# The query projection of a two-part decode attention kernel: unrolled matmuls against a loop with register addresses

## The chip, the cores and the metric

The kernel runs on one core of a Trainium2 chip. The metric is device time in microseconds (us) of one execution. A trace is one profiled execution; its span is about 1.5 us shorter than the time of the same run (245.4 against 246.84 us in the kernel before). Ratios are the mean time of one kernel's fast runs over the mean of the other's fast runs of the same rounds, so they differ a little from the ratio of the medians that stand beside them.

## The reference

Two independent attention layers for one new token, A and B. A sees only the last 2048 keys of its cache, B sees all 8192. The outputs are concatenated.

```python
# x: 1 x 576, wq: 576 x 4096, caches: 16 heads x 8192 x 128, wo: 4096 x 576, all bf16
q = (x @ wq).reshape(32 heads, 128)
k, v = the cache (A: its last 2048 rows), each head used by two query heads
p = softmax(q @ k.T * 128 ** -0.5)
out = (p @ v).reshape(4096) @ wo
```

Nearly all of the bytes are K and V (B: 64 MiB, A: 16 MiB) and the four weight matrices (4.5 MiB each). Each byte is loaded once.

## The kernel before

Five groups of K and V (group 0 is A, groups 1 to 4 are B) pass through four SBUF slots of 4 MiB each: two for K, two for V. SyncE issues all large loads into one queue. Ahead of the groups stand the two query projections. Their weights borrow slots that the groups will need: B's wq covers the second K slot, so the load of A's second K half may be issued only when the last q matmul of B has read its weights.

```python
    WQ = [(4 * SLOT - WQ_W, [("v", 0, 1), ("v", 1)]),                       # A's wq: in the V slots
          (SLOT, [("k", 1, 0), ("k", 1, 1), ("v", 0, 0)])]                  # B's wq: in the second K slot
    for P in range(2):
        off, res = WQ[P]
        x_columns(P)                 # VectorE spreads x over the weight columns of the matmuls
        load(slots[:, off:off + WQ_W], ... wqs[P] ..., res, "wq%d" % P)
        q_part(P, off, res)          # 36 matmuls
        q_finish(P)                  # ScalarE copy, 4 small matmuls, VectorE copy
    # (cut)
    for g in range(NG):              # NG = 5
        for s in range(2):
            load_kv(ks, g, s, koff(s), KS[s], "k")
        # (cut: V loads, transposes of K, scores, softmax, V, all on TensorE in one loop over g)
```

One q part, before the change:

```python
    def q_part(P, off, res):
        def mm(pe):
            for u in range(9):
                for j in range(4):
                    o = off + u * 2048 + j * 512
                    ins = pe.matmul(opsum[32 * j:32 * j + 32, P * 512:(P + 1) * 512], lhsT=xpad[:, P, u, :],
                                    rhs=slots[:, o:o + 512], start=(u == 0), stop=(u == 8))
            return ins
        add("pe", mm, reads=[("xpad", P)] + res, writes=[B_O[P]])
```

## Time and profile before

| | before |
|---|---|
| time, median | 247.23 us in 3 runs before the prediction; 247.14 us with the 3 runs beside the changed kernel |
| bytes moved | 102.8 MB at 419 GB/s |
| TensorE (PE) busy | 67% of the span |
| q matmuls of B end, second K load issued | 26.8 us, 26.83 us |
| packets, in order of start, reach the last byte of the first K half (about where the queue would have ended) | 33.86 us |

From the page of the kernel before: busy tenths of PE and of the DMA engines in 40 slices of 6.1 us each, the bytes moved per slice, and the head of the chain of waits that ended last.

```profile
PE   0006329993836999443999390999671699859684
...
DMA  9998999999999999999999999999999999999993
GB/s 349 421 445 383 426 425 421 418 418 419 469 419 433 438 423 427 427 438 427 427 434 443 438 433 433 427 427 427 433 433 427 433 438 433 427 445 427 403 416 140
...
DMA 8%; PE 3%; DVE 0%; SPq 0%; issue 0%
```

The DMA engines work all the time, and the chain ends in a load. PE has gaps everywhere. The kernel takes as long as its bytes take, so PE work is free as long as it never lets the queue run empty (run 10 below: the transposes start 8.8 us later, the queue stays full, and the time is 246.87 us).

The timeline of PE around the q parts (start, duration, engine, line, operation, output<-inputs, count, idle time before and what ended it). Line 433 is the q part, 444 its small follow-up, 472 the transposes of the first K half.

```profile
17.79 0.17 PE L415 MATMUL misc<-xnine,twice 64*128 64x18 bf16 x1 [17.79 <-DMA xnine<-in_B_x_dram]
18.77 4.03 PE L433 MATMUL opsum<-slots,xpad 128*32 128x512 bf16 x36 [0.81 <-DVE xpad L424]
23.50 0.26 PE L444 MATMUL misc<-selq,qrow 128*128 128x8 bf16 x4 [0.70 <-ACT qrow L439]
24.66 2.13 PE L433 MATMUL opsum<-slots,xpad 128*32 128x512 bf16 x36 [0.91 <-DMA slots<-in_B_wq_dram]
...
35.07 2.18 PE L472 MATMUL ktps<-ident,slots 128*128 128x128 bf16 x19 [7.33 <-PEq L214]
```

After q, PE idles for 7.3 us at its wait in line 214: it waits for the first K half, whose last packets are only then on their way. The timeline of SyncE shows how the DMA queue is fed:

```profile
26.83 2.48 SPq L404 DMA_DIRECT2D slots<-in_A_k_cache_dram  x4
29.36 12.76 SPq L404 DMA_DIRECT2D slots<-in_A_v_cache_dram  x8
```

The issue at 26.83 us comes right after the last q matmul. The queue had work until about 33.9 us at that moment, so several microseconds were in hand.

### The profile page before, as it was taken

Reading aid. Unit: us, or ns where it says so; the run is one execution under the profiler, and the core shown is the slowest. Engines: PE = TensorE matmul, PEld = TensorE weight load, DVE = VectorE, ACT = ScalarE, POOL = GpSimd, SP = SyncE. Lnnn points to the kernel's source line nnn. Section 1 sums busy time; section 2 is a strip of 40 time slices with the busy share of each in tenths; the row PEclk is TensorE's granted clock in tenths of the full one; section 3 lists DMA queues with packets and bytes.
Section 4 is the critical chain, followed back from the end, with each engine's and each line's share of the span. In section 5 each row is a group of like instructions: output and inputs, shape, how many; then the busy total and the mean of one; then the engine's idle time right before and its main releaser. Section 6 shows DMA issues by size and latency. Waiting matters only on the chain. (4 is left out here: it accounts for less than half of the span.)

```text
span 245.4 us, 5175 instructions
## 1 busy us (share of the span) xinstructions
PE 165.1 (67%) x2285; PEld 117.5 (48%) x2285; DVE 87.2 (36%) x148; ACT 87.4 (36%) x95; POOL 10.7 (4%) x48
## 2 busy tenths in 40 slices
PE   0006329993836999443999390999671699859684
PEld 0002129781316876213877130978330687625463
DVE  0001205654142465250556323355524256533311
ACT  2000016873003786101778200577600378610000
POOL 7400000000000000000000000000000000000000
PEclk9999957999575999795899866599979599975679
DMA  9998999999999999999999999999999999999993
GB/s 349 421 445 383 426 425 421 418 418 419 469 419 433 438 423 427 427 438 427 427 434 443 438 433 433 427 427 427 433 433 427 433 438 433 427 445 427 403 416 140
DMA packets 5796, 102.87 MB, mean 419 GB/s; under 512 B 794, under 2 KB 924, under 8 KB 1180
## 3 DMA queue, kind: packets, MB, share of 16 engines
q1 hardware_dynamic: 5628, 102.77, 98.2%
q8 instruction: 5, 0.08, 0.1%
q10 hardware_dynamic: 160, 0.00, 0.0%
q14 instruction: 3, 0.02, 0.0%
HBM read 102.76 MB, written 0.00 MB: 419 GB/s over the span
## 5 line engine op out<-in xcount | busy, mean ns | idle before, releaser
L478 ACT ACTIVATE kt<-ktps 128x1024 bf16<-128x1024 bf16 x80 | 78.5, 1022 | 95.1 <-PE ktps L472 94.9
L472 PE MATMUL ktps<-ident,slots 128*128 128x128 bf16 x1280 | 89.1, 236 | 34.1 <-PEq L214 34.1
L472 PEld LDWEIGHTS ktps<-ident,slots 128*128 128x128 bf16 x1280 | 83.2, 107 | 49.7 <-issue 49.7
L481 DVE COPY kt<-ktps 128x1024 bf16<-128x1024 bf16 x80 | 55.3, 692 | 74.1 <-PE ktps L472 74.1
L546 PE MATMUL opsum<-slots,ptm 128*32 128x512 bf16 x320 | 32.0, 557 | 5.1 <-PEq L214 5.1
L493 PE MATMUL sacc<-kt,qst 128*32 128x512 bf16 x320 | 25.4, 392 | 1.9 <-PEq L214 1.9
L546 PEld LDWEIGHTS opsum<-slots,ptm 128*32 128x32 bf16 x320 | 13.0, 127 | 18.9 <-issue 16.8
L557 DVE TENSOR_TENSOR vtmp<-opsum,maskV 128x512 f32<-128x512 f32 x8 | 5.5, 692 | 22.6 <-PE opsum L546 22.6
L415 PE MATMUL misc<-xnine,twice 64*128 64x18 bf16 x1 | 0.2, 173 | 17.8 <-DMA xnine<-in_B_x_dram 17.8
L524 PE MATMUL misc<-ident,psb 128*128 128x128 bf16 x40 | 3.3, 230 | 11.6 <-PEq L214 11.6
L462 POOL COPY qst<-qcol 128x8 bf16<-128x8 bf16 x20 | 3.1, 191 | 163.7 <-PE sacc L493 149.3
L439 ACT ACTIVATE qrow<-opsum 128x512 bf16<-128x512 f32 x2 | 1.2, 597 | 22.7 <-PE opsum L433 22.7
L524 PEld LDWEIGHTS misc<-ident,psb 128*128 128x128 bf16 x40 | 2.5, 101 | 14.0 <-issue 14.0
L640 PE MATMUL ktps<-slots,opj 128*32 128x144 bf16 (+1 forms) x192 | 8.3, 271 | 1.1 <-DMA slots<-in_B_wo_dram 1.1
L514 ACT ACTIVATE psb<-sacc,stat 128x1024 bf16<-128x1024 f32 x5 | 5.6, 1114 | 9.5 <-DVE stat L508 9.5
L493 PEld LDWEIGHTS sacc<-kt,qst 128*32 128x32 bf16 x320 | 5.0, 94 | 7.9 <-issue 4.3
L415 PEld LDWEIGHTS misc<-xnine,twice 64*128 64x128 bf16 x1 | 0.1, 103 | 17.8 <-issue 17.8
L533 DVE TENSOR_SCALAR ptm<-misc,par 128x512 bf16<-128x512 bf16 x10 | 4.4, 480 | 10.4 <-PE misc L524 10.4
L640 PEld LDWEIGHTS ktps<-slots,opj 128*32 128x32 bf16 x192 | 6.2, 104 | 3.1 <-DMA slots<-in_B_wo_dram 1.5
L384 DVE TENSOR_REDUCE acc<-vtmp 128x128 f32<-128x1024 f32 x4 | 7.5, 1872 | 0.1
L433 PE MATMUL opsum<-slots,xpad 128*32 128x512 bf16 x72 | 6.2, 504 | 1.7 <-DMA slots<-in_B_wq_dram 0.9
L424 DVE TENSOR_SCALAR xpad<-misc,par 128x5 bf16<-128x5 f32 (+1 forms) x8 | 1.2, 230 | 14.0 <-PE misc L415 14.0
(65 smaller groups left out, 41.2 us busy)
## 6 DMA issues: line engine op xcount, KB each, us to landing
slots<-in_B_k_cache_dram SPq DMA_DIRECT2D x8, 4096.0 KB
slots<-in_B_v_cache_dram SPq DMA_DIRECT2D x8, 4096.0 KB
slots<-in_A_k_cache_dram SPq DMA_DIRECT2D x8, 1024.0 KB
slots<-in_A_v_cache_dram SPq DMA_DIRECT2D x8, 1024.0 KB
slots<-in_A_wq_dram SPq DMA_DIRECT2D x1, 4608.0 KB, 13.6
slots<-in_B_wq_dram SPq DMA_DIRECT2D x1, 4608.0 KB, 23.7
slots<-in_A_wo_dram SPq DMA_DIRECT2D x1, 4608.0 KB, 19.2
slots<-in_B_wo_dram SPq DMA_DIRECT2D x1, 3024.0 KB, 26.0
```

Of the source, the lines that this page charges most:

```text
L384: add("dve", lambda dve: dve.tensor_reduce(out, view, AX.X, ALU.add), reads=reads, writes=writes, tag=tag)
L433: ins = pe.matmul(opsum[32 * j:32 * j + 32, P * 512:(P + 1) * 512], lhsT=xpad[:, P, u, :], rhs=slots[:, o:o + 512], start=(u == 0), stop=( ...
L472: ins = pe.matmul(ktps_bf[q][:, t * 128:(t + 1) * 128], lhsT=slots[:, o:o + 128], rhs=ident[:, :], start=True, stop=True, is_transpose=True)
L478: add("act", lambda act, q=q, dst=dst: act.activation(dst, ktps_bf[q], ACT.Copy), reads=[("bank", q)], writes=[("kt", u % NKT, q)], tag="e ...
L481: add("dve", lambda dve, q=q, dst=dst: dve.tensor_copy(dst, ktps_bf[q]), reads=[("bank", q)], writes=[("kt", u % NKT, q)], tag="e%d%d" % ( ...
L493: ins = pe.matmul(sacc[32 * j:32 * j + 32, :], lhsT=qst[:, o:o + 32], rhs=rhs, start=(u == 0 and e == 0), stop=True, skip_group_check=True)
L514: return act.activation(psb[:, :].rearrange("p (x g) -> p x g", g=2), src, ACT.Exp, bias=st(C_NB + g), scale=SCALE, accum_out=st(C_L + g))
L524: ins = pe.matmul(dst[:, t * 128:(t + 1) * 128], lhsT=psb[:, t * 128:(t + 1) * 128], rhs=ident[:, :], start=True, stop=True, is_transpose= ...
L533: ins = dve.tensor_scalar(to, src, par2[:, e:e + 1], None, ALU.mult)
L546: ins = pe.matmul(opsum[32 * j:32 * j + 32, s * 512:(s + 1) * 512], lhsT=ptm[:, o:o + 32], rhs=v[:, :, b:b + 128], start=(tt == 0), stop=( ...
L557: add("dve", lambda dve: dve.tensor_tensor(vtmp[:, 4 * s:4 * s + 4, :], src, by, ALU.mult), reads=[B_O[s], w], writes=[("vtmp", s)], tag=" ...
L640: ins = pe.matmul(ktps[P][32 * j:32 * j + 32, 0:w], lhsT=opj[:, P, jj:jj + 32], rhs=slots[:, o:o + w], start=(jj == 0), stop=(jj == HQ - 1))
```

## The change

Intent: a shorter PE program. Seven of the nine units of each q part run as passes of a loop, whose weight and data addresses are computed into registers. The first and the last unit stay static, because they carry the flags and the signal. The output address is always static; the helper takes a static matmul and gives it the inputs of a register-addressed one.

```diff
+    def by_register(pe, second):
+        block = nc.cur_bb.bb.instructions
+        first = block.pop()
+        second()
+        other = block.pop()
+        return pe.add_instruction(copy.replace(first, ins=other.ins, name=nc.get_next_instruction_name()))
+
     def q_part(P, off, res):
+        def one(pe, j, part, w, x, start):
+            return pe.matmul(opsum[part:part + 32, P * 512:(P + 1) * 512], lhsT=w, rhs=x[:, j * 512:(j + 1) * 512],
+                             start=start, stop=True, skip_group_check=True)
+
         def mm(pe):
-            for u in range(9):
+            w, x = xpad[:, P, :, :].rearrange("p u c -> p (u c)"), slots[:, off:off + WQ_W]
+            for j in range(4):
+                one(pe, j, 32 * j, w[:, 0:32], x[:, 0:2048], True)
+            with pe.Fori(1, 8) as u:
+                wu, xu = w[:, bass.ds(u * 32, 32)], x[:, bass.ds(u * 2048, 2048)]
                 for j in range(4):
-                    o = off + u * 2048 + j * 512
-                    ins = pe.matmul(opsum[32 * j:32 * j + 32, P * 512:(P + 1) * 512], lhsT=xpad[:, P, u, :],
-                                    rhs=slots[:, o:o + 512], start=(u == 0), stop=(u == 8))
+                    one(pe, j, 32 * j, w[:, 0:32], x[:, 0:2048], False)
+                    by_register(pe, lambda: one(pe, j, 0, wu, xu, False))
+            for j in range(4):
+                ins = one(pe, j, 32 * j, w[:, 8 * 32:9 * 32], x[:, 8 * 2048:9 * 2048], False)
             return ins
```

## The prediction

> **What bounds the kernel now.** The DMA engines. The page's DMA row reads 9 in nearly every slice, 102.8 MB move at 419 GB/s, and the chain of waits ends in an 18.5 us transfer of B_wo. TensorE is busy 67%: work on it costs nothing until it leaves the DMA queue empty.

> **Where the q matmuls stand.** In the timeline, the 36 matmuls of q for A run from 18.8 to 22.8 us (0.107 us apart[...]), those of B from 24.66 to 26.79 us (0.059 us apart). Only then may the second half of A's K be loaded, because B's wq lies in those slots: SyncE issues it at 26.83 us. Until then the queue holds only the rest of A's first K half, whose last packet ends at 33.86 us (packet records). The kernel's first packets came 1.0 us after their issue. So the end of q for B can slip by about 5.7 us for free. What it slips beyond that is DMA idle time, and as the queue never runs dry afterwards, it comes out one for one at the end.

> **What the change removes.** 96 static weight loads and matmuls, less 20 added instructions: about 10 per q part, of which 4 are the loop's own and about 6 compute addresses. Static instructions are cheap: the sequencer passed some 72 between 18.74 and 19.62 us, 12 ns each. The trace has five 16 KB instruction fetches on one queue, 1 us each; none repeats per pass of the outer loop and none delays the chain. I expect no gain.[...]

> **What it adds.** Seven passes per q part. The outer loop's records price control: register move to next move 0.103 us, add to branch 0.10 us, taken branch to the next record 0.27 us: 0.47 us per pass. Six more register operations at 0.10 us: 0.6 us. Eight register-addressed instructions (4 weight loads, 4 matmuls): nothing in this trace has such an operand[...]. Sum about 1.5 us per pass (0.9 to 2.2), against 0.43 or 0.24 us of array time now. The sequencer sets the pace.

> **On the critical path.** q for A ends at 18.75 + 0.2 + 7 x 1.5 + 0.5 = 30 us; q for B starts 1.85 us later (as now) and ends at about 43 us. The K issue moves from 26.8 to 43 us; DMA idles from 33.9 to about 44: some 10 us.

> **Prediction.** 257.5 us, 80% range 248.5 to 267. Faster by over 2%: 3%; within 2%: 20%; slower by over 2%: 77%.

> **What would show each step.** The DMA row falls to near 0 for a slice or two around 34 to 44 us. Each q part shows groups of 4 matmuls about 1.5 us apart. SyncE's second K issue is near 43 us. PE's transposes start near 44 instead of 35.07 us. From 80 us on all is shifted by one constant.

> **What would make it wrong.** A pass under 0.8 us: the slack swallows it and the time stays at 247. Fewer address operations[...].[...]

The sum in "What it adds" came to about 1.5 us per pass, the two terms that stand make 0.47 + 0.6 = 1.07 us, and the rest, about 0.43 us, was for the eight register-addressed instructions, of which the trace before had none.

## The result, and the profile after

The changed kernel takes 250.76 us (median of 6 runs, 250.54 to 251.08), the kernel before 247.14 us (6 runs): ratio 1.0141, 95% interval 1.0125 to 1.0157. It is slower, by about a third of what was forecast.

The same rows of the page of the changed kernel (slices of 6.2 us):

```profile
PE   0008679499442999490999580799764599859684
...
DMA  9998949999999999999999999999999999999993
GB/s 331 426 461 376 425 176 389 418 427 424 423 449 452 436 422 425 420 425 425 467 416 441 425 425 425 420 462 425 441 425 425 420 425 436 452 446 408 422 415 135
...
DMA 7%; PE 3%; DVE 0%; SPq 0%; issue 0%
```

One slice stands out: the sixth of the DMA row, 31 to 37 us, reads 4 where 9 stood, and 176 GB/s. The rest looks as before. The timelines of PE and of SyncE show the cause; line 440 is the q part now, 491 the transposes.

```profile
19.13 4.23 PE L440 MATMUL opsum<-slots,xpad 128*32 128x512 bf16 x20 [0.81 <-DVE xpad L426]
23.59 0.76 PE L440 MATMUL opsum<-slots,xpad 128*32 x4 [0.23 <-issue]
24.60 0.76 PE L440 MATMUL opsum<-slots,xpad 128*32 x4 [0.26 <-issue]
25.59 1.06 PE L440 MATMUL opsum<-slots,xpad 128*32 x8 [0.23 <-issue]
...
34.94 1.06 PE L440 MATMUL opsum<-slots,xpad 128*32 x8 [0.24 <-issue]
...
36.99 0.22 PE L491 MATMUL ktps<-ident,slots 128*128 128x128 bf16 x1
```

```profile
36.04 2.48 SPq L406 DMA_DIRECT2D slots<-in_A_k_cache_dram  x4
38.57 6.72 SPq L406 DMA_DIRECT2D slots<-in_A_v_cache_dram  x8
```

The groups of four matmuls start 1.0 us apart, with 0.23 to 0.26 us in between in which PE waits for nothing that the profile shows ("issue"); the records of PE's sequencer, shown further below, fill that time. B's part ends at 36.0 us instead of 26.8, and the second K load is issued at 36.04 us. The stretches of both traces around it (length, busy time and count of each engine, granted PE clock, DMA share, GB/s), before and then after:

```profile
30.00:34.00 4.00, 0.00 (x0) 0.00 (x0) 0.00 (x0) 0.00 (x0) 0.00 (x0) 0.50 1.01 422
34.00:38.00 4.00, 2.93 (x28) 2.96 (x29) 0.69 (x1) 1.20 (x2) 0.00 (x0) 0.50 1.02 426
```

```profile
30.00:34.00 4.00, 3.52 (x17) 1.55 (x16) 0.00 (x0) 0.00 (x0) 0.00 (x0) 0.69 0.92 381
34.00:38.00 4.00, 3.02 (x35) 1.99 (x36) 0.98 (x5) 0.96 (x2) 0.00 (x0) 1.00 0.20 43
38.00:42.00 4.00, 4.00 (x68) 3.30 (x66) 3.24 (x5) 3.51 (x4) 0.00 (x0) 1.00 1.00 406
```

Between 34 and 38 us the DMA engines moved 43 GB/s instead of 426. The packet records give the edges: the last packet of the first K half ends at 34.67 us, the next load's first packet starts at 37.36 us. Counting landed bytes, the changed kernel reaches 13.7 MB 4.2 us later than the kernel before (38.20 against 34.03 us), 40 MB 4.1 us later, 90 MB 4.0 us later and 102 MB 4.1 us later. So the whole loss arises in this one gap, and none of it is made up or added to afterwards. (The profiled run of the changed kernel was its slowest, 251.08 us, and that of the kernel before a quick one, 246.84 us; hence 4.1 us here against 3.6 us between the medians.)

### The profile page after: what moved, and what is told of

Same layout as the page of the kernel before. It is cut to its first block, busy times and chain, and to the rows that moved or that the text cites. A ratio compares the mean times of both kernels' runs of the same rounds, so it can differ in the third digit from the quotient of the medians.

```text
span 249.5 us, 5275 instructions
## 1 busy us (share of the span) xinstructions
PE 170.1 (68%) x2285; PEld 117.7 (47%) x2285; DVE 87.0 (35%) x148; ACT 87.0 (35%) x95; POOL 10.7 (4%) x48
## 5 line engine op out<-in xcount | busy, mean ns | idle before, releaser
L491 PE MATMUL ktps<-ident,slots 128*128 128x128 bf16 x1280 | 86.2, 232 | 31.3 <-PEq L216 31.3
L491 PEld LDWEIGHTS ktps<-ident,slots 128*128 128x128 bf16 x1280 | 80.2, 105 | 46.7 <-issue 46.5
L440 PE MATMUL opsum<-slots,xpad 128*32 (+1 forms) x72 | 13.4, 475 | 3.4 <-DVE xpad L426 1.7
L543 PE MATMUL misc<-ident,psb 128*128 128x128 bf16 x40 | 4.0, 261 | 11.5 <-PEq L216 11.5
L440 PEld LDWEIGHTS opsum<-slots,xpad 128*32 (+1 forms) x72 | 5.9, 96 | 10.4 <-issue 9.1
L543 PEld LDWEIGHTS misc<-ident,psb 128*128 128x128 bf16 x40 | 3.0, 115 | 14.0 <-issue 14.0
L659 PEld LDWEIGHTS ktps<-slots,opj 128*32 128x32 bf16 x192 | 5.7, 103 | 3.5 <-DMA slots<-in_B_wo_dram 2.2
```

Of the source, the lines that this page charges most:

```text
L440: return pe.matmul(opsum[part:part + 32, P * 512:(P + 1) * 512], lhsT=w, rhs=x[:, j * 512:(j + 1) * 512], start=start, stop=True, skip_gro ...
L491: ins = pe.matmul(ktps_bf[q][:, t * 128:(t + 1) * 128], lhsT=slots[:, o:o + 128], rhs=ident[:, :], start=True, stop=True, is_transpose=True)
L543: ins = pe.matmul(dst[:, t * 128:(t + 1) * 128], lhsT=psb[:, t * 128:(t + 1) * 128], rhs=ident[:, :], start=True, stop=True, is_transpose= ...
L659: ins = pe.matmul(ktps[P][32 * j:32 * j + 32, 0:w], lhsT=opj[:, P, jj:jj + 32], rhs=slots[:, o:o + w], start=(jj == 0), stop=(jj == HQ - 1))
```

## The experiments

The theory: a q part delays only the issue of the second K load. Up to a limit this is free; beyond it the queue is empty and every microsecond counts. From the result, the limit is an issue at about 32.2 us (36.04 less 3.6 to 4.1). Rivals: each loop costs its share wherever it stands; taken branches are dear; matmuls with register addresses are dear; the shifted program costs time in other stages, by fetches.

The comparison with the reference called all ten runs correct, also the four with a wrong q (twice, fixed_address, fresh, apart_fresh). So it is blind to q here and proves nothing about the register addresses. Each group of runs shared its runs of the kernel before: medians 246.98 us (runs 1 to 4), 247.00 us (5 to 8) and 246.91 us (9 and 10).

### 1 and 2: one loop at a time

In loop_a, B's part is static; in loop_b, A's is (the condition is then `P == 0`).

```diff
         def mm(pe):
+            if P == 1:
+                # the nine static units, as in the kernel before
+                return ins
             w, x = xpad[:, P, :, :].rearrange("p u c -> p (u c)"), slots[:, off:off + WQ_W]
```

> Only A's q part runs in the loop; B's is unrolled as before. Theory (slack): a delay of the second K issue costs nothing until the queue runs dry; the changed kernel issued it at 36.0 us and lost 3.6 to 4.1 us, so the free limit is an issue at about 32.2 us. Here q for A ends near 26.3 us, q for B near 31 us (30 to 32.1), the K issue follows at once: loss 0 to 0.2 us, time 247.2 us, no gap in the DMA records. Rival (each loop costs its half, wherever it stands): 249.0 us.

Measured: 247.69 us (4 runs, 246.98 to 247.81), ratio 1.002, interval 1.0004 to 1.0037. The K issue came at 30.32 us and the DMA engines were never all idle there, though between 33.5 and 35 us only 311 GB/s landed (431 in the kernel before).

> Only B's q part runs in the loop. Theory (slack): q for B starts at 24.6 us and takes 7.5 us, the K issue is at about 32.1 us, just at the limit of 32.2 us: loss 0 to 0.3 us, time 247.2 to 247.5 us. Rival (half each): 249.0 us.

Measured: 247.24 us (247.09 to 247.28), ratio 1.001, interval 0.9993 to 1.0026. The K issue came at 32.30 us.

What follows: half the loops do not cost half the loss. One loop delays the K issue from 26.83 us by 3.5 us (loop_a) or 5.5 us (loop_b) and costs about 0.5 or 0.2 us by the ratios; two delay it by 9.2 us and cost 3.6 us. That is a threshold, but not a sharp one. loop_a was expected to lose at most 0.2 us and lost about 0.5 us (interval 0.1 to 0.9), more than loop_b, whose issue was later. Its trace reaches 13.7 MB 0.35 us late, without a gap. The same small delay stands in loop_b (0.41 us) and in run 7, no_loop (0.35 us), and at 102 MB all three are still 0.37 or 0.38 us late; run 8, two_units, shows only 0.07 us, although its issue was later than that of loop_a. What loop_a's trace loses beyond loop_b's arises in the last 0.1 MB of the queue. Neither is explained.

### 3 and 4: no K load waits for q of B

B's wq moves into the buffer of the transposed keys, which is unused until the q parts are over (it grows by 4 KiB per partition). The diff is abridged: the matmuls of B also read their weights from there. Done to the kernel before (apart_before) and to the changed one (apart_after).

```diff
-    kt = nc.alloc_sbuf_tensor("kt", [128, NKT, UNIT], BF16)
+    ktw = nc.alloc_sbuf_tensor("ktw", [128, WQ_W], BF16)
+    kt = ktw[:, 0:NKT * UNIT].rearrange("p (a y) -> p a y", a=NKT)
...
-    WQ = [..., (SLOT, [("k", 1, 0), ("k", 1, 1), ("v", 0, 0)])]
+    WQ = [..., (None, [("kt", u, q) for u in range(NKT) for q in range(4)] + ["ktw"])]
...
-        load(slots[:, off:off + WQ_W], ...
+        load(slots[:, off:off + WQ_W] if P == 0 else ktw[:, :], ...
```

> The kernel before, with B's wq in the buffer of the transposed keys (free until the q parts are over), so that no K load waits for q. Theory: the queue was never dry there anyway, so nothing is gained: 247.1 us (246.8 to 247.4). All K and V loads that wait for q parts now wait for A's part at most.

Measured: 247.00 us (246.85 to 247.29), ratio 1.0005, interval 0.9988 to 1.0021.

> The changed kernel with the same move of B's wq. Theory (the whole loss is the DMA gap at the second K load): gap gone, second K issue within the first 8 us, time as apart_before within 0.4 us: 247.2 us, though q for B still ends at 36 us. Rival (the loop or the shifted code costs time elsewhere, in fetches or in PE stages): stays near 250.7 us, or between.

Measured: 246.86 us (246.82 to 246.92), ratio 0.9995 to the kernel before, interval 0.9979 to 1.0012. Its q loops are as slow as ever. The timeline of PE in apart_after (line 441 is the q part, 492 the transposes), and its stretch of 34 to 38 us:

```profile
34.66 1.07 PE L441 MATMUL opsum<-ktw,xpad 128*32 x8 [0.24 <-issue]
36.42 0.26 PE L464 MATMUL misc<-selq,qrow 128*128 128x8 bf16 x4 [0.70 <-ACT qrow L459]
36.72 3.92 PE L492 MATMUL ktps<-ident,slots 128*128 128x128 bf16 x64
```

```profile
34.00:38.00 4.00, 3.02 (x40) 2.05 (x38) 1.25 (x5) 1.24 (x2) 0.00 (x0) 1.00 1.01 422
```

What follows: with the same loops, the same shorter program and q of B again ending near 36 us, but with the K load issued at 3.88 us, the loss is gone. The gap in the queue is the whole loss. The shorter program neither costs nor gains anything that these intervals (0.17% each way) can show.

### 5: each register-addressed matmul twice

```diff
-                for j in range(4):
+                for j in (0, 1, 2, 3, 0, 1, 2, 3):
```

> Wrong result on purpose: each pass of both loops issues its four register-addressed matmuls twice. In the changed kernel's trace one such matmul takes 0.124 us of the sequencer, so a pass should grow from 1.02 to 1.52 us, the value the prediction had used. Theory: 14 passes, so the K issue moves by 7.0 us from 36.0 to 43 us and the time by as much: 257.7 us (256.9 to 258.5). Rival (part of a longer gap is made up later): below 256 us.

Measured: 250.85 us (250.81 to 251.03), ratio 1.0158. The expectation failed, and the failure is the most telling result. The group of line 440 in the changed kernel, then in twice (PEldq is PE's sequencer):

```profile
L440 PEld LDWEIGHTS opsum<-slots,xpad x72: 91/93/103, 19.1 to 35.6; 128*32 x56, 128*32 128x32 bf16 x16
...
L440 PEldq FUSED_REGOPS  x56: 42/46/51, 19.4 to 35.2; - x56
```

```profile
L440 PEld LDWEIGHTS opsum<-slots,xpad x128: 92/93/112, 18.8 to 35.4; 128*32 x112, 128*32 128x32 bf16 x16
...
L440 PEldq FUSED_REGOPS  x56: 42/46/51, 19.1 to 35.1; - x56
```

There are 56 more matmuls, but the same 56 register operations: the second four matmuls found their addresses ready in registers. The mean distance between a pass's branch and the next is 1.017 us in both traces. So fifty-six extra matmuls with register addresses cost no measurable time. What costs is computing a fresh address; run 9 tests that.

### 6: the loop with constant addresses

```diff
-                wu, xu = w[:, bass.ds(u * 32, 32)], x[:, bass.ds(u * 2048, 2048)]
                 for j in range(4):
-                    one(pe, j, 32 * j, w[:, 0:32], x[:, 0:2048], False)
-                    by_register(pe, lambda: one(pe, j, 0, wu, xu, False))
+                    one(pe, j, 32 * j, w[:, 32:64], x[:, 2048:4096], False)
```

> Wrong result on purpose: both loops stay, but their matmuls have constant addresses, so no register operation but the count and the branch is left. Sum of records: add 0.10, branch 0.27, eight static instructions 0.10: a pass of 0.45 to 0.5 us. K issue near 29 us, under the limit of 32.2 us: 247.1 us. Rival (a taken branch is dear by itself[...]): passes near 1 us, 249 us or more.

Measured: 247.05 us (246.84 to 247.16), ratio 0.9999. A pass took 0.38 to 0.42 us in the records, less than expected, and the K issue came at 28.39 us. In A's part that is no longer than the four matmuls took in the kernel before (4 x 0.107 = 0.43 us). In B's part they had taken 4 x 0.059 = 0.24 us, so the loop costs something there, but the issue is only 1.56 us later and stays within the slack. The branch alone is harmless here.

### 7: register addresses without a loop

```diff
-            with pe.Fori(1, 8) as u:
+            count = pe.alloc_register("count%d" % P)
+            pe.reg_mov(count, 1)
+            for k in range(7):
+                u = pe.snap(count, min_val=1, max_val=7)
                 # (wu, xu and the four matmuls as in the changed kernel)
+                pe.reg_add(count, count, 1)
```

> Right result: both parts unrolled, but each of the 7 middle units takes its addresses from a register, as in the changed kernel. No branch: a unit should take 0.62 to 0.75 us. K issue at 30.5 to 32 us, at or under the limit: 247.1 to 247.4 us. Rival (register-addressed matmuls are dear[...]): 1.0 us per unit and 249.5 us or more.

Measured: 247.12 us (247.04 to 247.26), ratio 1.0006, interval 0.9989 to 1.0023. A unit took 0.70 to 0.74 us (one took 0.88), the upper end of what was expected: the first register operation of a unit, which by the author's reading takes in the count, lasted 142 to 153 ns instead of 78. The K issue came at 32.29 us, a little later than expected, at the limit. So neither the loop alone nor the addresses alone cost the 3.6 us; only their sum crosses the limit.

### 8: two units per pass

```diff
-            with pe.Fori(1, 8) as u:
-                wu, xu = w[:, bass.ds(u * 32, 32)], x[:, bass.ds(u * 2048, 2048)]
+            with pe.Fori(1, 7, 2) as u:
+                for k in range(2):
+                    wu, xu = w[:, bass.ds(u * 32 + 32 * k, 32)], x[:, bass.ds(u * 2048 + 2048 * k, 2048)]
...
-            for j in range(4):
-                ins = ...                        # unit 8
+            for k in range(7, 9):
+                for j in range(4):
+                    ins = ...                    # units 7 and 8
```

> Right result: the loop runs 3 passes of 2 units, one more unit is static; the program is still shorter than before, by about half as much. A pass: 1.02 us plus four matmuls at 0.124 us, about 1.52 us, so a part costs 3 x 1.52 instead of 7 x 1.02 us. K issue near 31.7 us, under the limit of 32.2 us: 247.2 us (247.0 to 247.6). Rival (any loop there costs): 249 us or more.

Measured: 246.96 us (246.66 to 247.18), ratio 0.9997, interval 0.9981 to 1.0014. A pass took 1.55 us, the K issue came at 31.67 us. This keeps a good part of the shortening (20 of 36 matmuls per part in the program instead of 12) at no cost. It does not beat the kernel before; no version here does, and none is to be expected to by this route, since the queue was never empty before.

### 9 and 10: longer passes, with fresh addresses

Because run 5 had not lengthened the pass, four matmuls with four new addresses were added to each.

```diff
                     by_register(pe, lambda: one(pe, j, 0, wu, xu, False))
+                next = x[:, bass.ds(u * 2048 + 2048, 2048)]
+                for j in range(4):
+                    one(pe, j, 32 * j, w[:, 0:32], x[:, 0:2048], False)
+                    by_register(pe, lambda: one(pe, j, 0, wu, next, False))
```

> Wrong result on purpose. The run twice left a pass at 1.02 us, because its second four matmuls reused the address registers: it measured a register-addressed matmul as free, not the pass as longer. Here each pass has four more matmuls with four fresh addresses (the next unit's columns), so four more fused register operations of 0.124 us with their matmul, as in two_units, where they made a pass of 1.55 us. Theory: pass 1.52 to 1.55 us, K issue 7.2 us later than 36.0, near 43.3 us, and the time later by as much: 257.9 us (257.0 to 258.8). Rival (part of a longer gap is made up later): below 256 us.

Measured: 257.64 us (257.49 to 257.69), ratio 1.0434, interval 1.0417 to 1.0451. A pass took 1.52 us on the mean, 0.50 us more than in twice: 0.125 us for each matmul whose address is fresh, where those of twice, with ready addresses, had cost nothing. The K issue came at 42.81 us. Against twice, the issue moved by 6.78 us and the time by 6.79 us (6.88 us when each is taken against its own runs of the kernel before). The group of line 440 in fresh has twice the register operations, and the page shows the longer gap:

```profile
L440 PEldq FUSED_REGOPS  x112: 42/46/51, 19.1 to 42.0; - x112
...
42.81 2.48 SPq L406 DMA_DIRECT2D slots<-in_A_k_cache_dram  x4
```

```profile
DMA  9999921999999999999999999999999999999993
GB/s 351 415 432 398 427 107 22 425 412 423 427 468 427 414 409 462 435 409 445 450 416 414 450 435 420 414 455 435 414 445 445 420 414 455 430 427 455 400 408 150
```

> Wrong result on purpose: the same long passes, with B's wq in the buffer of the transposed keys, so that no K load waits for q of B. q for B ends near 43 us, seven us later than in apart_after, and the transposes start near 44 us. Theory (the DMA gap at the second K load is the whole loss): the queue has K and V of A to move until 60 us and stays full: 247.0 us (246.8 to 247.5). Rival (a late PE costs by itself): 3 us or more over apart_after.

Measured: 246.87 us (246.75 to 247.01), ratio 0.9997, interval 0.9981 to 1.0014. q for B ended near 43 us here too, and the transposes began at 43.86 us, 8.8 us later than in the kernel before. With the queue full, this cost nothing.

## Why the prediction was wrong, point by point

- **The mechanism held.** The kernel is bound by its DMA queue; the q part of B gates the second K load; the loss is one gap in the queue, carried to the end unchanged. Runs 3, 4, 9 and 10 show each of these links.
- **The slack was right in its sum, with some luck.** The prediction said 5.7 us, an issue at 32.5 us. Two other runs give 32.2 us (twice: 36.03 less its loss of 3.85 us) and 32.1 us (fresh: 42.81 less 10.73 us). But its parts were off: its own figures make 33.86 - 1.0 - 26.83 = 6.0 us, and it doesn't say what took 0.3 us off. In the changed kernel the refill took 1.32 us from issue to first packet, not 1.0, and this happens to be the missing 0.3 us. Nor is 33.86 us a sharp end: there, 3 packets were still under way at 34.0 us, where the kernel before had 17, and the last one ended at 34.67 us.
- **The step that failed is the price of a pass**: "Sum about 1.5 us per pass". It is 1.02 us. These are the sequencer's records of one pass of the changed kernel, as start in us, duration in ns and operation:

```
20.964  36 ALU_OP            add to the loop count
21.061 212 COMPARE_BRANCH
21.332  78 FUSED_REGOPS      \
21.468  42 FUSED_REGOPS       } address operations; the next three stand between the matmuls
21.560 102 LDWEIGHTS         (its matmul follows)
21.588  46 FUSED_REGOPS
21.684 100 LDWEIGHTS
21.713  46 FUSED_REGOPS
21.808 103 LDWEIGHTS
21.837  46 FUSED_REGOPS
21.933  98 LDWEIGHTS
21.961  36 ALU_OP            the next pass
```

| per pass | predicted | from the starts of these records |
|---|---|---|
| control: count and taken branch | 0.47 us | 0.37 us (no separate register move; it had been counted from the outer loop) |
| address operations | 6 x 0.10 = 0.6 us | five fused ones: 0.136 + 0.092 + 0.096 + 0.095 + 0.096 = 0.52 us |
| four weight loads and matmuls with register addresses | the rest of the sum, about 0.43 us | 4 x 0.028 = 0.11 us; in twice, the last of these 0.028 us holds five weight loads and matmuls instead of one |
| sum | 1.5 us | 1.00 us (mean over a part: 1.02 us) |

- The large error is the third line: about 0.43 us was put down, 0.11 us measured; this one term makes 0.32 us of the difference of 0.50 us. The trace before had no such instruction, so the term was not measured in this case. Run 5 shows that it was too high: 56 additional matmuls with register addresses changed a pass by less than 1 ns. The prediction had measured 12 ns per static instruction in the same trace; eight of those are 0.1 us, which would have been the better guess.
- **The error was multiplied.** There are 14 passes in a row, and beyond the limit everything counts: 14 x (1.5 - 1.02) = 6.7 us, and 257.5 - 6.7 = 250.8 us, which is the measured time. Conversely fresh, whose passes take 1.52 us, takes 257.64 us.
- **The range held, the odds did not.** 250.76 us lies within 248.5 to 267, but "slower by over 2%" had 77%, and the time grew by 1.4%. A threshold turns a third less per pass into two thirds less loss; the range allowed for that, the middle of it didn't.
- **No gain from the shorter program**, as predicted: apart_after against the kernel before is 0.9995 (0.9979 to 1.0012). No branch of a pass stood out: the passes of run 6 took 0.38 to 0.42 us, branch included. But these branches go back over a few instructions only. Branches of PE's later loop over the groups vary more: the fourth one recorded there took 2.49 us in fixed_address and 1.92 us in apart_after, where a 16 KB fetch (about 1 us) had begun 0.03 and 0.60 us before it, and 0.21 to 0.44 us in the other traces. No run tests the cause, and these two runs lost no time by it (247.05 and 246.86 us). The change left the number of 16 KB instruction fetches at five in both traces.
- **The signs to look for** had the same error of size. The DMA row fell to 4 in one slice, not to near 0; the groups of four stand 1.0 us apart, not 1.5; the K issue came at 36.04 us, not near 43; the transposes start at 36.99 us, not near 44. In fresh, with its longer passes, the row falls to 2 and 1, and the issue is at 42.81 us.

## What to carry to other kernels

When a load waits for an engine, compute how long the queue behind it lasts: that was the engine's slack here (an issue at about 32.2 us was the limit). Up to there the cost was near zero (0 to 0.5 us in the last 2 us before the limit), and beyond it every microsecond counted (fresh against twice: the issue 6.78 us later, the time 6.79 us longer). A register address cost its computation, not its use: each matmul with a fresh address lengthened a pass by 0.125 us (fresh), those with ready addresses by nothing measurable (twice, 1.017 us per pass as without them). So share addresses between instructions and take more work per pass (two units in one pass took 1.55 us, in two passes 2 x 1.02 us). And if a buffer's reuse sits on the limit, moving the buffer (here into one that is idle at that time) takes the whole question away (apart_after: 246.86 us against 250.76).
